# Rotating Strassen products over six PSUM tiles, starting two blocks of each group early, and moving the first batch's normaliser sums to another bank

## Chip, core and metric

The kernel runs on one core of one Trainium2 chip. The metric is the device time of one execution in microseconds (us). The kernel before was timed three times: 1553.96, 1553.99 and 1556.23 us, median 1553.99 us.

## What is computed

Attention with normalised queries and keys (8 batches, 12 heads, 448 positions, head size 64), and then a two-layer feed-forward with SiLU on the joined heads (3584 tokens, 768 to 2048 to 768). Everything is float32.

```python
q_n, k_n = rmsnorm(q, g_q), rmsnorm(k, g_k)
scores = (q_n @ k_n.T) / sqrt(64)
attn = exp(scores - max); attn = attn / (sum(attn) + 1e-9)
x = (attn @ v), heads joined: (3584, 768)
h = x @ w_in;  g = h * sigmoid(h);  out = g @ w_out
```

## The kernel before

The work is written out by hand in one order (a manual schedule), so every engine executes its instructions in the order in which the Python code emits them. Two arms are built; the data of this case takes the arm `bounded`.

**Pairs.** Batch and head pair give 48 pairs `n` (6 per batch `b`, numbered `hp` inside it). The main loop (L780) runs n = 0 to 48; n = 48 has no pair and only finishes. For each pair the loop emits, on TensorE: the first half of its scores (`scores(n, 0)`, L400), the second half of the weighted sum of the pair ahead (`weigh(n - 1, 1)`, L416), the transposes of the next queries (L381), a portion of filler work (`fill`, L803), the sums that normalise the pair ahead (`divide(n - 1)`, L445), the second half of the scores, the first half of the weighted sum, the transposes of the next keys (L386), and again filler (L841). ScalarE computes the exponentials (L405), copies transposed queries out of PSUM (L382), scales transposed keys of the first two batches (L390) and copies products; VectorE adds the exponentials (`add_up`, L430, L433), takes the reciprocal (L449), scales later keys (L392) and adds products (L459). GpSimd raises to a power (L304) and multiplies (L308, L451 for batch 0).

**Filler.** The first layer of the feed-forward is spread over the pairs as a generator: `begin(work, columns, parts)` sets a share of `columns / parts`, and each `fill()` emits matmuls until that share is used up. Batches 0 and 1 have eight of their blocks computed plainly (`whole`, L552, 6 matmuls a block); everything else goes by groups of two batches in Strassen-like blocks of seven products (`Seven`, L511), in the order 1, 2 (`two`) and 6, 5, 7, 3, 4 (`five`). Products 1 and 2 use the raw attention output; the others use sums that VectorE makes with `sum_x` (L456). A product's result is added or copied out of PSUM right after its last matmul, but the instruction for that is only emitted when the generator is resumed, which can be in the next portion. Rows of `stage` hold results; there are three such buffers, each block takes two.

**After the pairs.** The last group (batches 6 and 7) has no pairs beside it and runs alone (`alone = True`, L799), while `w_out` is loaded and rounded beside it (`prepare_out`, L674, instructions at L83, L84, L106 to L117). Then the second layer runs over 14 tiles of 256 tokens, again with seven products each (`halves_out`, L702).

**PSUM.** There are eight banks: two tiles `mm`, two tiles `sc` of two banks each (the scores of two heads), one `tr` (transposes and `divide`), one `av`. Beside pairs a product takes an `mm` tile. When alone, `bank()` (L481) walks through eight banks: mm, mm, sc half 0, sc half 1, sc half 0, sc half 1, tr, av; the two halves of an `sc` tile belong to one tile object.

Of the kernel before, what the change touches and what calls it, by code (L numbers as in the profile page):

```python
# [27 lines left out]
BANK = 512  # L28
# [296 lines left out]
def bounded(  # L325
# [112 lines left out]
    def divide(n):  # L438


        t = ps.tile([P, S], F32, name="tr")
        sums = [es, es_two] if n < z.NPAIR else [es]
        for i, part in enumerate(sums):
            for h in range(2):
                nc.tensor.matmul(  # L445
                    t[ds(h * D, D), :], ones[0:R, :], part[:, h, :],
                    start=i == 0, stop=i == len(sums) - 1,
                )
        nc.vector.reciprocal(out=r, in_=t)  # L449
# [284 lines left out]
    def fill(most=None):  # L734
        filler["due"] += filler["share"]
        while filler["due"] > 0 and most != 0:
            filler["due"] -= next(filler["work"], filler["due"])
            most = most and most - 1
# [3 lines left out]

    def finish():
        for _ in filler["work"]:
            pass
# [34 lines left out]
    for n in range(last + 2):  # L780
# [5 lines left out]
        if n > 0:  # L786
# [3 lines left out]
            unload(n - 1)  # L790
        transpose(n + 1, "q")
        if n == 0:
            normalise(2)
        if ends and n <= last:
            begin(halves_in([b - 2, b - 1], range(HF), plain), products,
                  4 * NPAIR - (2 if b == z.B - 2 else 1))
        weights_in(n, 0)
        if n > last:
            alone = True  # L799
            for _ in begun[1][1].two():  # L800
                pass
        else:
            fill(2 * HW if ends else None)  # L803
        weights_in(n, 1)
        if n == last:

            finish()
            rows = [staged() for _ in range(2)]
            begun = [(rows, part_in([b - 1, b], 0, rows))]
            rows = [staged(), work[:, 0 : 2 * S]]  # L810
            begun.append((rows, part_in([b - 1, b], 1, rows, kT)))
        if n > 0:
            divide(n - 1)
        if n <= last:
            scores(n, 1)
            weigh(n, 0)
        transpose(n + 1, "k")
        if n <= last:
            add_up(n, 1)
        if ends:  # L820
            sum_x([b - 2, b - 1], HW - 1)
            if n > last:
                begin(halves_in([b - 2, b - 1], range(HF), prepare_out, begun), 1, 1)
        elif hp == 0 and b == 1:
            begin(whole(0, early), len(early) * z.NW * S, 2 * NPAIR - 1)
        elif hp == 0 and b == 2:
            columns = len(early) * z.NW * S + products // 2
            begin(first_two(), columns, 4 * NPAIR - 2)
        weights_in(n, 2)
        if b % 2 == 1 and b > 1 and hp == NPAIR - 1:  # L830
            finish()
            for c in range(HW - 1):
                sum_x([b - 1, b], c)
            if n == last:
                for _ in begun[0][1].two():
                    pass
# [3 lines left out]
        elif n <= last:  # L840
# [220 lines left out]
```

## Time and profile before

The profiled execution took 1553.03 us, of which the instruction span is 1551.2 us.

| Part of the span (us) | What runs | Length | TensorE busy |
|---|---|---|---|
| 0 to 95.9 | start and batch 0, no filler | 95.9 | 68.3 |
| 95.9 to 860 | pairs with filler | 764.1 | 748.0 |
| 860 to 1016.9 | last group alone | 156.9 | 139.0 |
| 1016.9 to 1551.2 | second layer | 534.3 | 512.3 |

A float32 matmul stands in the trace as two records. A time in square brackets at a timeline row is the idle time of the engine ahead of the row and what ended it. `PEclk` is the clock that TensorE was granted, 1.00 being full.

### The profile page before, as it was taken

What the parts mean: (1) busy time and instruction counts of PE and PEld (TensorE: products, weight loads), DVE (VectorE), ACT (ScalarE), POOL (GpSimd) and SP (SyncE); (2) the same over time, 40 slices, a digit from 0 to 9 for tenths busy, and PEclk for the clock granted to TensorE, in tenths of its full rate; (3) what the DMA queues carried; (4) which work ended last, traced back from release to release, by engine and by line L of the source; (5) the groups of instructions that cost most, each with busy time, mean ns of one, the idle gap of its engine ahead of it and who ended that gap; (6) DMA issues with size and microseconds to landing.
All of it is one profiled execution on the core that took longest, in us unless ns stands there. A gap on an engine that the chain in (4) does not pass through costs nothing.

```text
span 1551.2 us, 14002 instructions
## 1 busy us (share of the span) xinstructions
PE 1467.5 (95%) x5072; PEld 704.4 (45%) x5072; DVE 739.8 (48%) x928; ACT 565.7 (36%) x931; POOL 393.7 (25%) x250
## 2 busy tenths in 40 slices
PE   5899999999899999899999989989999999999998
PEld 2334344434344444344444334455555555555554
DVE  4777776665755555755554766621211111222220
ACT  5778777444455454455454443300000000000000
POOL 5665341333233333313322133310000000000000
PEclk9999999999999999999999999999999999999999
DMA  6324332211222221222221246322222222222220
GB/s 199 106 67 139 109 99 66 66 60 54 60 84 60 60 83 60 60 66 71 60 72 36 77 164 210 119 78 74 75 75 80 75 80 75 75 76 85 81 68 23
DMA packets 119187, 128.94 MB, mean 83 GB/s; under 512 B 48836, under 2 KB 101316, under 8 KB 119108
## 3 DMA queue, kind: packets, MB, share of 16 engines
q1 hardware_dynamic: 118788, 127.95, 26.8%
q8 instruction: 42, 0.69, 0.2%
q14 instruction: 37, 0.30, 0.1%
q10 hardware_dynamic: 320, 0.00, 0.0%
HBM read 87.56 MB, written 40.37 MB: 82 GB/s over the span
## 4 chain that ended last, share of the span: by engine, by line
PE 84%; DVE 6%; issue 2%; ACT 1%; DMA 0%; POOL 0%; ACTq 0%; DVEq 0%; POOLq 0%
PE mm L511 28%; PE sc L511 19%; PE sc L400 9%; PE av L416 8%; PE tr L511 5%; PE av L511 5%; PE mm L552 5%; PE tr L445 3%; PE tr L386 1%; PE tr L381 1%; DVE work L433 1%; DVE sums_x L456 1%; DVE stage L459 1%; DVE parts L459 1%; DVE rms L298 0%
## 5 line engine op out<-in xcount | busy, mean ns | idle before, releaser
L405 ACT ACTIVATE work<-sc,rms 112x448 f32<-112x448 f32 x384 | 212.0, 635 | 226.9 <-PE sc L400 148.2
L304 POOL TENSOR_TENSOR rms<-rms,minus_half 112x16 f32<-112x16 f32 (+1 forms) x49 | 175.9, 3590 | 329.1 <-DVE rms L300 312.3
L511 PE MATMUL mm<-x,W 128*128 128x448 f32 x552 | 220.6, 542 | 1.3 <-DVE stage L459 0.9
L531 POOL TENSOR_TENSOR parts<-parts 128x448 f32<-128x448 f32 (+1 forms) x42 | 45.8, 1090 | 639.7 <-DVE parts L459 639.7
L449 DVE RECIPROCAL work<-tr 128x448 f32<-128x448 f32 x48 | 142.0, 2958 | 123.9 <-PE tr L445 112.5
L400 PE MATMUL sc<-work 64*112 64x448 f32 x768 | 173.0, 570 | 7.1 <-ACT work L390 4.7
L416 PE MATMUL av<-work,rows 112*64 112x448 f32 x768 | 165.5, 552 | 0.0
L511 PE MATMUL mm<-sums_x,W 128*128 128x448 f32 x384 | 157.0, 543 | 7.5 <-DVE stage L459 3.5
L433 DVE TENSOR_TENSOR work<-work 112x896 f32<-112x896 f32 x132 | 147.2, 1115 | 1.6
L511 PEld LDWEIGHTS mm<-x,W 128*128 128x128 f32 x552 | 101.8, 190 | 94.3 <-issue 87.2
L400 PEld LDWEIGHTS sc<-work 64*112 64x112 f32 x768 | 62.4, 176 | 107.4 <-issue 90.1
L511 PEld LDWEIGHTS mm<-sums_x,W 128*128 128x128 f32 x384 | 70.1, 190 | 73.0 <-issue 56.6
L511 PE MATMUL sc<-W,work 128*128 128x384 f32 x288 | 96.8, 486 | 0.0
L416 PEld LDWEIGHTS av<-work,rows 112*64 112x64 f32 x768 | 46.6, 136 | 109.0 <-issue 107.0
L459 DVE TENSOR_TENSOR stage<-mm,parts 128x448 f32<-128x448 f32 (+1 forms) x73 | 44.8, 617 | 104.2 <-PE mm L511 67.5
L459 DVE TENSOR_TENSOR parts<-mm,parts 128x448 f32<-128x448 f32 (+1 forms) x50 | 30.7, 613 | 112.4 <-PE mm L511 112.1
L552 PE MATMUL mm<-x,W 128*128 128x448 f32 x192 | 75.6, 541 | 0.0
L518 ACT COPY parts<-sc 128x384 f32<-128x384 f32 (+1 forms) x11 | 5.4, 493 | 190.6 <-PE sc L511 190.6
L511 PEld LDWEIGHTS sc<-W,work 128*128 128x128 f32 x288 | 54.8, 190 | 38.1
L459 DVE TENSOR_TENSOR parts<-sc,parts 128x384 f32<-128x384 f32 (+1 forms) x22 | 12.9, 584 | 104.5 <-PE sc L511 104.4
L405 ACT ACT_TABLE_LOAD x36 | 46.2, 1283 | 39.9 <-issue 36.9
L445 PE MATMUL tr<-work,ones 112*64 112x448 f32 x192 | 47.3, 572 | 13.3 <-ACT work L382 7.8
(146 smaller groups left out, 1883.6 us busy)
## 6 DMA issues: line engine op xcount, KB each, us to landing
hidden<-stage SPq DMA_DIRECT2D x55, 448.0 KB, 3.0
work<-hidden SPq DMA_DIRECT2D x7, 2048.0 KB, 9.4
x<-hidden SPq DMA_DIRECT2D x7, 2048.0 KB, 8.7
W<-in_moe_w_in_dram SPq DMA_DIRECT2D x24, 512.0 KB, 3.8
rows<-in_moe_w_out_dram SPq DMA_DIRECT2D x32, 384.0 KB, 3.8
rows<-in_q_dram SPq DMA_DIRECT2D x48, 224.0 KB, 3.5
rows<-in_k_dram SPq DMA_DIRECT2D x48, 224.0 KB, 3.3
rows<-in_v_dram SPq DMA_DIRECT2D x48, 224.0 KB, 2.6
```

Of the source, the lines that this page charges most:

```text
L304: nc.gpsimd.tensor_tensor(out=flat, in0=flat, in1=half, op=ALU.pow)
L381: nc.tensor.transpose(t[:, ts(j, R)], rows[:, j, :], ident[0:R, 0:R])
L400: nc.tensor.matmul(banks[:, h, 0:S], kT[rows, ts(j, R)], qT[n % 2][rows, :], start=True, stop=True,)
L405: nc.scalar.activation(e[j][:, h, :], banks[:, h, 0:S], AF.Exp, scale=rms[n % 4][:, 1, h, j : j + 1])
L416: nc.tensor.matmul(st["av"][ds(h * D, D), :], st["v"][:, h, j, :], e[j][:, h, :], start=(j == 0), stop=(j == J - 1),)
L433: nc.vector.tensor_tensor(out=es, in0=e[0] if j == 1 else es, in1=e[j], op=ALU.add)
L445: nc.tensor.matmul(t[ds(h * D, D), :], ones[0:R, :], part[:, h, :], start=i == 0, stop=i == len(sums) - 1,)
L449: nc.vector.reciprocal(out=r, in_=t)
L459: nc.vector.tensor_tensor(out=out, in0=a, in1=b, op=ALU.add)
L511: nc.tensor.matmul(t, self.left(name, s), self.right(name, s), start=s == ends[0], stop=s == ends[1])
L531: nc.gpsimd.tensor_tensor(out=u2, in0=u2, in1=p5, op=ALU.add)
L552: nc.tensor.matmul(h, room.w1(c, f), xT(b, c), start=(c == 0), stop=(c == z.NW - 1))
```

## The change

Four edits, in the order of the diff.

1. `divide` takes a `bank` (an `mm` tile, free in batch 0) in place of `tr` for the pairs of the first batch.
2. `bank()` in the alone stages walks through six tiles: mm, mm, sc, sc, tr, av. Of an `sc` tile only the first of the two banks is used.
3. For the groups that run beside pairs, `start` makes the first two blocks ahead: the products 1 and 2 of block 0 are emitted in the first portion of the group's first pair, ahead of `divide` (with their additions), and the products 1 and 2 of block 1 at the place of its second portion. `halves_in` goes on from there with the five other products. The first portion of `sum_x` stays at the end of the pair ahead, the second moves from there into the group's first pair. Block 1 keeps product 1 in the free half of its own row in place of `kT`, and its second row is a `stage` row.
4. The shares change: the plain blocks of batch 0 are spread over 12 portions in place of 11 (4 matmuls each), `first_two` over 23 in place of 22, the groups over 22 and 21 for 156 matmuls in place of 23 and 22 for 168. In batch 0 the transposes of the next keys are emitted ahead of the first half of the weighted sum.

```diff
     def divide(n):
-        t = ps.tile([P, S], F32, name="tr")
+        t = ps.tile([P, S], F32, name="tr") if n >= z.NPAIR else bank(S)
...
     alone = False
-    free_banks, shared = [], {}
+    order = ["mm", "mm", "sc", "sc", "tr", "av"]
 
     def bank(n):
         if not alone:
             return ps.tile([P, BANK], F32, name="mm", bufs=2)[:, 0:n]
-        if not free_banks:
-            free_banks.extend([("mm", [P, BANK], None)] * 2)
-            free_banks.extend([("sc", [P, 2, BANK], i) for i in range(2)] * 2)
-            free_banks.extend((name, [P, S], None) for name in ("tr", "av"))
-        name, shape, half = free_banks.pop(0)
-        if half != 1:
-            bufs = 2 if name in ("mm", "sc") else 1
-            shared["bank"] = ps.tile(shape, F32, name=name, bufs=bufs)
-        t = shared["bank"]
-        return t[:, 0:n] if half is None else t[:, half, 0:n]
+        name = order[0]
+        order.append(order.pop(0))
+        if name == "sc":
+            return ps.tile([P, 2, BANK], F32, name=name, bufs=2)[:, 0, 0:n]
+        if name == "mm":
+            return ps.tile([P, BANK], F32, name=name, bufs=2)[:, 0:n]
+        return ps.tile([P, S], F32, name=name)[:, 0:n]
...
-                columns, skip = part.five(int(m == 0)), 5 * (HW - 1) if m == 0 else 0
+                late = int(alone and m == 0)
+                columns, skip = part.five(late), 5 * (HW - late) * late
...
+    def start(group):
+        begun = []
+        for m in range(2):
+            rows = [staged() for _ in range(2)]
+            begun.append((rows, part_in(group, m, rows, rows[0][:, S:] if m else None)))
+        return begun
...
             unload(n - 1)
+            if ends and n <= last:
+                sum_x([b - 2, b - 1], 1)
         transpose(n + 1, "q")
...
+        weights_in(n, 0)
         if ends and n <= last:
-            begin(halves_in([b - 2, b - 1], range(HF), plain), products,
-                  4 * NPAIR - (2 if b == z.B - 2 else 1))
-        weights_in(n, 0)
-        if n > last:
+            begun = start([b - 2, b - 1])
+            run(begun[0][1].two())
+        elif n > last:
             alone = True
-            for _ in begun[1][1].two():
-                pass
+            run(begun[1][1].two())
         else:
-            fill(2 * HW if ends else None)
+            fill()
...
         if n <= last:
             scores(n, 1)
+        if b == 0:
+            transpose(n + 1, "k")
+        if n <= last:
             weigh(n, 0)
-        transpose(n + 1, "k")
+        if b > 0:
+            transpose(n + 1, "k")
...
             sum_x([b - 2, b - 1], HW - 1)
+            group = [b - 2, b - 1]
             if n > last:
-                begin(halves_in([b - 2, b - 1], range(HF), prepare_out, begun), 1, 1)
+                run(halves_in(group, range(HF), prepare_out, begun))
+            else:
+                run(begun[1][1].two())
+                begin(halves_in(group, range(HF), plain, begun), products - 4 * HW * S,
+                      4 * NPAIR - (3 if b == z.B - 2 else 2))
         elif hp == 0 and b == 1:
-            begin(whole(0, early), len(early) * z.NW * S, 2 * NPAIR - 1)
+            begin(whole(0, early), len(early) * z.NW * S, 2 * NPAIR)
         elif hp == 0 and b == 2:
             columns = len(early) * z.NW * S + products // 2
-            begin(first_two(), columns, 4 * NPAIR - 2)
+            begin(first_two(), columns, 4 * NPAIR - 1)
...
-            for c in range(HW - 1):
-                sum_x([b - 1, b], c)
+            sum_x([b - 1, b], 0)
             if n == last:
-                for _ in begun[0][1].two():
-                    pass
+                sum_x([b - 1, b], 1)
+                run(begun[0][1].two())
...
-        elif n <= last:
+        elif not ends:
             fill()
```

The order of instructions moves as follows; `L511` before and `L508` after are the same line, a product's matmul.

TensorE in batch 0, before: from the transposes of one pair's keys to the scores of the same pair's second half (`tr`, `sc`, `av`, `mm` are PSUM tiles, `rows` and `qn` the loaded and normalised inputs).

```order
L386 MATMUL tr<-ident,rows 128x112 x4
L400 MATMUL sc<-work 112x448 x4
L416 MATMUL av<-work,rows 64x448 x4
L381 MATMUL tr<-ident,qn_103 128x112 x4
L445 MATMUL tr<-work,ones 64x448 x2
L445 MATMUL tr<-stage,ones 64x448 x2
L400 MATMUL sc<-work 112x448 x4
```

The same place in the changed kernel, from the second half of the scores of the pair ahead.

```order
L400 MATMUL sc<-work 112x448 x4
L386 MATMUL tr<-ident,rows 128x112 x4
L416 MATMUL av<-work,rows 64x448 x4
L400 MATMUL sc<-work 112x448 x4
L416 MATMUL av<-work,rows 64x448 x4
L381 MATMUL tr<-ident,qn_103 128x112 x4
L445 MATMUL mm<-work,ones 64x448 x2
L445 MATMUL mm<-stage,ones 64x448 x2
```

A weighted sum (L416) now stands between the key transposes and the scores that use the keys, and the sums of `divide` (L445) no longer write the tile that the query transposes have just filled.

TensorE around the start of group 2, 3 (n = 23 to 24), before, from the key transposes at the end of pair 23.

```order
L386 MATMUL tr<-ident,rows 128x112 x4
L400 MATMUL sc<-work 112x448 x4
L416 MATMUL av<-work,rows 64x448 x4
L381 MATMUL tr<-ident,qn_103 128x112 x4
L511 MATMUL mm<-x_144,W 128x448 x6
L445 MATMUL tr<-work,ones 64x448 x2
L400 MATMUL sc<-work 112x448 x4
L416 MATMUL av<-work,rows 64x448 x4
L386 MATMUL tr<-ident,rows 128x112 x4
L511 MATMUL mm<-sums_x,W 128x448 x6
```

The same place in the changed kernel.

```order
L386 MATMUL tr<-ident,rows 128x112 x4
L508 MATMUL mm<-x_143,W 128x448 x2
L508 MATMUL mm<-sums_x,W 128x448 x3
L400 MATMUL sc<-work 112x448 x4
L416 MATMUL av<-work,rows 64x448 x4
L381 MATMUL tr<-ident,qn_103 128x112 x4
L508 MATMUL mm<-x_144,W 128x448 x6
L445 MATMUL tr<-work,ones 64x448 x2
L400 MATMUL sc<-work 112x448 x4
L416 MATMUL av<-work,rows 64x448 x4
L386 MATMUL tr<-ident,rows 128x112 x4
L508 MATMUL mm<-x_144,W 128x448 x6
```

Five matmuls of the group ahead now stand between the key transposes and the scores, and the second portion of pair 24 uses raw outputs (`x_144`) and no longer sums (`sums_x`).

TensorE at the start of the second layer, before, with tile numbers: four products in a row of the first token tile (`x0_143` and `W_75` hold weights, `work_148` the tokens).

```order
L511 MATMUL mm_4800<-x0_143,work_148 128x384 x2
L511 MATMUL mm_4800<-W_75,work_148 128x384 x6
L511 MATMUL sc_4810<-x0_143,work_148 128x384 x2
L511 MATMUL sc_4810<-W_75,work_148 128x384 x6
L511 MATMUL sc_4810<-x0_143,work_148 128x384 x2
L511 MATMUL sc_4810<-W_75,work_148 128x384 x6
L511 MATMUL sc_4831<-x0_143,work_148 128x384 x2
L511 MATMUL sc_4831<-W_75,work_148 128x384 x6
```

Products at the same stage in the changed kernel.

```order
L508 MATMUL mm_4794<-x0_143,work_148 128x384 x2
L508 MATMUL mm_4794<-W_75,work_148 128x384 x6
L508 MATMUL sc_4804<-x0_143,work_148 128x384 x2
L508 MATMUL sc_4804<-W_75,work_148 128x384 x6
L508 MATMUL sc_4814<-x0_143,work_148 128x384 x2
L508 MATMUL sc_4814<-W_75,work_148 128x384 x6
L508 MATMUL tr_4824<-x0_143,work_148 128x384 x2
L508 MATMUL tr_4824<-W_75,work_148 128x384 x6
```

Two products in a row shared the tile object `sc_4810`; now each product has one of its own, and the next tile to come round is six products away.

More of the change, by code (lines that the diff above doesn't have):

```diff
@@ L732, in begin, with fill, run @@
         filler.update(work=work, due=0.0, share=columns / parts)
-    def fill(most=None):
+    def fill():
         filler["due"] += filler["share"]
-        while filler["due"] > 0 and most != 0:
+        while filler["due"] > 0:
             filler["due"] -= next(filler["work"], filler["due"])
-            most = most and most - 1
     def plain(m):
         yield
+    def run(work):
+        for _ in work:
+            pass
     def finish():
-        for _ in filler["work"]:
-            pass
+        run(filler["work"])
+    def start(group):
[4 more added lines that the diff above has]
+        return begun
     early, late = range(z.NF // 2), range(HF // 2, HF)
@@ L807, in bounded @@
             finish()
[L808 to L811, printed above, removed]
+            begun = start([b - 1, b])
         if n > 0:
```

1 line of the change is left out of this document (removed).

## The prediction

> **What bounds the kernel now.** I read the stages first (busy time by windows), since the page's 95% of TensorE is a mean over unlike stages.
>
> ```profile
> span 1551.2 us, 14002 instructions
> ```
>
> ```profile
> 95.90:860.00 764.10, 748.02 (x2826) 317.27 (x2824) 472.85 (x560) 432.13 (x686) 252.70 (x136) 1.00 0.23 71
> ```
>
> ```profile
> 1016.92:1545.50 528.58, 512.27 (x1569) 296.03 (x1567) 103.91 (x126) 14.34 (x29) 27.24 (x28) 1.00 0.24 73
> 873.89:1016.92 143.03, 125.10 (x314) 60.03 (x313) 92.70 (x155) 49.87 (x90) 52.42 (x48) 0.96 0.44 143
> ```
>
> The columns are the length, then busy time and count of TensorE, its weight loads, VectorE, ScalarE and GpSimd, the granted clock, the DMA share and GB/s. Beside the pairs TensorE is busy 748 of 764 us. In the second layer it is busy 512 of 529 us while VectorE needs 104, and in the last group 125 of 143 us while VectorE needs 93. TensorE is the limit in all three, so each gap on it counts in full and no other engine fills a stage. The gaps are named by the view of waits, TensorE alone; first the last group (860 to 1017 us), then the second layer.
>
> ```profile
> PE sc L511 <- DVE stage L459: 9.8, 5, 4.2
> PE sc L511 <- DVE parts L459: 5.0, 5, 2.0
> PE sc L511 <- ACT parts L529: 1.9, 2, 1.3
> PE sc L511 <- ACT parts L518: 1.2, 2, 0.6
> ```
>
> ```profile
> PE sc L511 <- DVE stage L459: 4.2, 6, 0.7
> PE sc L511 <- DVE parts L459: 4.1, 6, 0.7
> PE sc L511 <- DVE W L459: 3.4, 5, 0.7
> PE sc L511 <- ACT parts L518: 2.4, 4, 0.6
> PE sc L511 <- ACT parts L529: 2.2, 3, 0.9
> ```
>
> Every wait of these two stages is on an `sc` tile: 14 waits with 17.9 us, and 24 with 16.3 us. None is on `mm`, `tr` or `av`. The same view over the whole run names the rest, all ahead of 860 us.
>
> ```profile
> PE tr L386 <- POOL rms L304: 12.2, 1, 12.2
> PE tr L445 <- ACT work L382: 7.8, 6, 2.0
> PE sc L400 <- ACT work L390: 4.7, 6, 0.8
> PE mm L511 <- DVE stage L459: 4.4, 5, 1.4
> PE tr L445 <- DVE W L106: 3.3, 1, 3.3
> PE mm L511 <- DVE sums_x L456: 2.9, 2, 1.5
> PE tr L445 <- DVE work L433: 2.2, 2, 1.1
> PE sc L400 <- DVE work L392: 1.7, 2, 0.9
> ```
>
> The first row is the start of the kernel, which the change leaves alone. Batch 0 loses 12.5 us (the second and third row); the fifth is one gap in pair 12; the other four are 11.2 us at the starts of the groups and in the filler of batches 2 and 3.
>
> **Second layer: one product for each `sc` tile.** The timeline of TensorE, one group of products:
>
> ```profile
> 1075.57 1.45 PE L511 MATMUL mm<-x,x 128*128 128x384 f32 x4
> 1080.73 1.46 PE L511 MATMUL sc<-x,sums_x 128*128 128x384 f32 x4
> 1086.78 1.56 PE L511 MATMUL sc<-x,x 128*128 128x384 f32 x4 [0.72 <-DVE stage L459]
> 1092.04 1.45 PE L511 MATMUL sc<-x,work 128*128 128x384 f32 x4
> 1097.97 1.56 PE L511 MATMUL sc<-x,work 128*128 128x384 f32 x4 [0.61 <-ACT parts L518]
> 1103.24 1.46 PE L511 MATMUL tr<-x,work 128*128 128x384 f32 x4
> ```
>
> ```profile
> 1086.16 0.56 DVE L459 TENSOR_TENSOR stage<-sc,parts 128x384 f32<-128x384 f32 x1 [4.62 <-PE sc L511]
> ```
>
> From `mm` to `sc` a product takes 1080.73 - 1075.57 = 5.16 us. The next, into the second half, starts 6.05 us later: it waits until the first half has been read at 1086.16 to 1086.72, though that read touches another bank. The order with tile numbers says why: both halves are one tile object (`sc_4810`). Four products from 1080.73 to 1103.24 take 22.51 us, where four of 5.16 are 20.64: 1.87 lost, more than the 1.33 of idle, because the first matmuls after a gap run 1.56 and not 1.45.
>
> The stage has 14 token tiles of 7 products, 98 in all (1569 records at 16 each). 98 x 5.16 = 505.7 us against 528.6 in the window: **22.9 us** go, if no new wait comes. In the new rotation a product waits for the reading of the one six before it, with five others in between, 5 x 5.16 = 25.8 us. The longest VectorE has to do in one piece there, the four sums of the next token tile, is far below that (104 us in 14 tiles, 7.4 us for everything). The lower end is 20, if an eighth of the gaps stays under another name.
>
> The Trainium skill ("TensorE: Matmul & The Clock Gate", section "A second HAM failure mode: psum-queue depth-cycling") says that frequent small idle spells between groups of matmuls, when products cycle through PSUM banks, make the clock oscillate between half and full. By that rule the products behind the 24 gaps would run at half speed now, and up to 24 x 5.16 = 124 us more would be won, an estimate from its rule and the product above. The trace does not agree: the row of this stage has the clock at 1.00 with all 24 gaps in it, and the sum goes by the row.
>
> **Last group.** 1569 and 314 records show the size: 52 products of six records. Unstalled neighbours:
>
> ```profile
> 890.82 2.42 PE L511 MATMUL mm<-sums_x,W 128*128 128x448 f32 x6
> 893.08 2.42 PE L511 MATMUL mm<-x,W 128*128 128x448 f32 x6
> 901.95 4.85 PE L511 MATMUL sc<-sums_x,W 128*128 128x448 f32 x6 [4.20 <-DVE stage L459]
> ```
>
> ```profile
> 908.07 0.62 DVE L459 TENSOR_TENSOR work<-sc,parts 128x448 f32<-128x448 f32 x1
> ```
>
> A product takes 2.26 us, so 52 take 117.5, and 25.5 us is the most to win. It exceeds the 17.9 us of idle because the product behind the longest gap ran 4.85 instead of 2.42. Here VectorE also rounds `w_out` and falls behind: block 1's last addition comes at 908.07 and ends at 908.7. That bank (`av`) is wanted again six products later. With five products begun at 873.9 and ten more, TensorE comes to it at 873.9 + 15 x 2.26 = 907.8: a wait of about 1 us. After that VectorE's 92.7 us in the window are below the 117.5 that TensorE needs, so it catches up. I take 2 us off for this and other remnants: **23.5 us**, between 12 (VectorE, ScalarE and the loads of `w_out` make a chain of their own) and 25.5.
>
> **Batch 0.** Two gaps a pair:
>
> ```profile
> 69.69 2.96 DVE L449 RECIPROCAL work<-tr 128x448 f32<-128x448 f32 x1 [2.84 <-POOL rms L304]
> 77.27 1.09 DVE L430 TENSOR_TENSOR stage<-work 112x896 f32<-112x896 f32 x1
> ```
>
> ```profile
> 79.35 0.97 PE L445 MATMUL tr<-work,ones 112*64 112x448 f32 x4 [1.16 <-ACT work L382]
> 80.15 0.92 PE L445 MATMUL tr<-stage,ones 112*64 112x448 f32 x4
> 81.00 1.76 PE L400 MATMUL sc<-work 64*112 64x448 f32 x8
> 90.86 0.97 PE L445 MATMUL tr<-work,ones 112*64 112x448 f32 x4 [1.17 <-ACT work L382]
> ```
>
> The 1.16 is `divide` waiting until ScalarE has copied the queries out of the one `tr` tile; an `mm` tile is free at once. The 0.78 (4.7 over six) is the scaling of the keys, now covered by a weighted sum. A pair lasts 90.86 - 79.35 = 11.51 us; without both gaps it would be 9.6. But then VectorE binds: from the reciprocal's start to the end of the addition that `divide` needs is 77.27 + 1.09 - 69.69 = 8.67 us, then the second half of `divide` (0.92) and two hand-overs of about 0.1: a circle of 9.8. So 1.7 a pair for four pairs, and about 3 for the first two, whose wait for `tr` was the longest (2.0): **10 us**, between 6 (a longer circle) and 12.5 (all idle).
>
> **Pair 12.** Eleven portions used up the plain blocks, and the twelfth was empty:
>
> ```profile
> 183.18 1.68 PE L445 MATMUL tr<-work,ones 112*64 112x448 f32 x4 [3.29 <-DVE W L106]
> 184.78 2.70 PE L400 MATMUL sc<-work 64*112 64x448 f32 x8
> ```
>
> Besides the 3.29, these rows took 1.68 and 2.70 where the same work took 0.97 and 1.76 above: 1.65 more. Twelve portions of 4 matmuls put 4 here (3 us), so I take **4.6 us** of 4.9, at least 3.
>
> **Starts of groups and filler.** The remaining four rows sum to 11.2 us. At pairs 24 and 36 the key scaling (1.7 for both) is covered by five or more filler matmuls; the wait for the exponentials' sums (2.2) goes since one portion of `sum_x` now stands behind them; the wait for `sum_x` (2.9) goes since the second portion needs no sums. The 4.4 for an `mm` tile come where a portion of filler ends exactly on a product, so that its addition is only emitted with the next portion; with 23 shares fewer do. I take **10**, between 0 (others appear, since the shares shift everything) and 11.2. The added `stage` row makes block 1 wait for block 0's store; that is how all later blocks work, and I cost it at nothing: five products lie between.
>
> **Sum.** 22.9 + 23.5 + 10 + 4.6 + 10 = 71.0 us from the profiled 1553.0: 1482.0. The median of the three runs lies 1.0 above that execution, so I forecast **1483 us**. All upper ends together (22.9 + 25.5 + 12.5 + 4.9 + 11.2 = 77.0) give 1477, and 1476 if matmuls behind a gap of batch 0 lost another 1 us as in pair 12. All lower ends together (41) give 1513; the causes are unrelated, so I take the half of it for the forecast's own range, 1494.
>
> **Rivals.**
>
> *The last group is set by another chain* (15 in 100). Rounding a piece needs its load, two ScalarE and three VectorE instructions, and additions queue between them. For it: the gap of 4.20 ended with VectorE late, not TensorE. Against: 93 of 143 us. If the stage gains 12 or less, the time is 1494 to 1506.
>
> *Fewer banks, more bubbles* (3 in 100). If the gaps came from the number of banks, six in place of eight would bring them 8/6 as often: 22.9 becomes 30.5 and 25.5 becomes 34, a loss of 16 against the other gains of 25, about 1545. It is also the case in which the change does not do what it says. Against: no gap at the single tiles `mm`, `tr` and `av`. The Trainium skill has that rule ("Perfetto Trace Analysis", section "Optimization Strategy": the same gap again and again can mean that there are too few buffers); the rows above do not agree with it here.
>
> *Slower: the clock* (2 in 100). If TensorE without gaps were granted less, the whole run stretches: each 0.01 costs 15 us, and below 0.95 it is slower than before; at 0.93 it is 1595. Against: 748 busy of 764 us at 1.00.
>
> The forecast has the remaining 80 in 100, its own range 1476 to 1494. With the first rival's nearer half the range is **1476 to 1500**. A measurement here tells apart about 0.2%, 3 us. Faster by more: 0.95; within: 0.02 (parts undone by waits not seen); slower: 0.03.
>
> **What would show it.** Right: no wait on `sc` L508 in the second layer and 5.16 us a product throughout; the last group's 52 products in about 119.5 us; in batch 0 reciprocals 9.8 us apart; no gap of 3 us at pair 12; under 3 us of waits of `mm`, `tr` and `sc` from 96 to 860 us. Wrong: gaps at `tr` or `av` tiles in the last group with VectorE late, or a clock below 1.00 in the second layer.

## The result and the profile after

The changed kernel takes 1479.2 us (median of four runs: 1476.25, 1479.0, 1479.38 and 1479.56), the kernel before beside it 1554.1 us (median of four). The ratio is 0.951, 95% interval 0.949 to 0.953: 4.9% faster, 74.9 us. The forecast was 1483 us in a range of 1476 to 1500.

The profiled execution of after is the fastest of the four, 1476.25 us. The stages are compared through it and the 1553.03 us of before, a difference of 76.8 us. The page and the view by windows of after, cut at the same places of the program as before (first filler product; first product of the stage alone; first product of the second layer; last product):

```profile
span 1474.5 us, 14016 instructions
```

```profile
84.64:844.08 759.44, 758.03 (x2867) 321.67 (x2865) 483.87 (x574) 441.93 (x699) 253.28 (x137) 1.00 0.24 75
```

```profile
32.17:84.64 52.47, 51.90 (x260) 18.53 (x261) 47.31 (x50) 42.60 (x81) 44.16 (x23) 1.00 0.38 102
844.08:962.74 118.66, 117.76 (x315) 59.28 (x314) 91.47 (x153) 48.89 (x89) 50.14 (x46) 1.00 0.53 169
962.74:1468.60 505.86, 505.84 (x1569) 297.98 (x1567) 105.33 (x129) 15.18 (x30) 29.46 (x30) 1.00 0.25 78
```

The same view of before, for batch 0 from 32.17 us on and for the pairs with filler (the table ahead of the prediction cuts both elsewhere):

```profile
32.17:96.30 64.13, 54.38 (x269) 19.81 (x265) 47.91 (x50) 43.25 (x81) 45.59 (x24) 0.97 0.32 89
96.30:873.89 777.59, 761.51 (x2867) 322.44 (x2865) 483.47 (x574) 440.49 (x699) 252.30 (x136) 1.00 0.24 73
```

| Stage (lengths in us) | Before | After | Gain | Forecast |
|---|---|---|---|---|
| start and batch 0, to the first filler product | 96.30 | 84.64 | 11.7 | 10 |
| pairs with filler | 777.6 | 759.4 | 18.2 | 14.6 (pair 12: 4.6; the rest: 10) |
| last group | 143.0 | 118.7 | 24.4 | 23.5 |
| second layer | 528.6 | 505.9 | 22.7 | 22.9 |

From the first filler product to the last product TensorE is busy 1381.6 of 1384.0 us, and the work of the other engines has hardly changed: VectorE's 92.7 us of the last group are 91.5 now. The gain is waiting time of TensorE, and in part matmuls that ran slowly behind a wait. The view of waits shows what is left of it, TensorE over the whole run of after:

```profile
PE tr L386 <- POOL rms L304: 12.3, 1, 12.3
PE tr L381 <- POOL qn L308: 1.6, 2, 1.3
PE av L508 <- DVE stage L459: 0.9, 1, 0.9
PE tr L381 <- ACT work L390: 0.8, 1, 0.8
PE mm L445 <- DVE stage L430: 0.8, 1, 0.8
PE mm L508 <- ACT parts L515: 0.6, 1, 0.6
...
```

The first row is the start, which the change leaves alone. No row names an `sc` tile with a product (L508). The one wait of the last group is on `av`, with 0.9 us. The timeline of TensorE in the second layer has 5.16 us from product to product, through `mm`, `sc`, `sc` and `tr` alike:

```profile
967.90 1.45 PE L508 MATMUL mm<-x,work 128*128 128x384 f32 x4
...
973.06 1.45 PE L508 MATMUL sc<-x,work 128*128 128x384 f32 x4
...
978.22 1.45 PE L508 MATMUL sc<-x,work 128*128 128x384 f32 x4
...
983.38 1.45 PE L508 MATMUL tr<-x,work 128*128 128x384 f32 x4
```

### The profile page after: what moved, and what is told of

It is laid out like the page before. It is cut to its first block, busy times and chain, and to the rows that moved or that the text cites. A ratio compares the mean times of both kernels' runs of the same rounds, so it can differ in the third digit from the quotient of the medians.

```text
span 1474.5 us, 14016 instructions
## 1 busy us (share of the span) xinstructions
PE 1449.3 (98%) x5072; PEld 703.8 (48%) x5072; DVE 739.8 (50%) x928; ACT 566.2 (38%) x931; POOL 393.4 (27%) x250
## 4 chain that ended last, share of the span: by engine, by line
PE 92%; DVE 5%; issue 1%; DMA 1%; ACT 0%; POOL 0%; ACTq 0%; SPq 0%; DVEq 0%; POOLq 0%
PE mm L508 35%; PE sc L508 13%; PE sc L400 9%; PE av L416 9%; PE av L508 7%; PE tr L508 7%; PE mm L549 5%; PE tr L445 3%; PE tr L386 1%; PE tr L381 1%; DVE work L449 1%; DVE rms L298 1%; DVE work L433 0%; DVE W L109 0%; DMA W<-in_moe_w_in_dram 0%
## 5 line engine op out<-in xcount | busy, mean ns | idle before, releaser
L304 POOL TENSOR_TENSOR rms<-rms,minus_half 112x16 f32<-112x16 f32 (+1 forms) x49 | 175.8, 3588 | 290.9 <-DVE rms L300 271.6
L508 PE MATMUL mm<-x,W 128*128 128x448 f32 x552 | 220.9, 541 | 0.7 <-ACT parts L515 0.6
L449 DVE RECIPROCAL work<-tr 128x448 f32<-128x448 f32 x42 | 124.2, 2957 | 104.5 <-PE tr L445 104.3
L400 PE MATMUL sc<-work 64*112 64x448 f32 x768 | 170.7, 563 | 1.0 <-ACT work L382 0.6
L508 PE MATMUL mm<-sums_x,W 128*128 128x448 f32 x408 | 165.9, 542 | 0.7 <-DVE stage L459 0.4
L416 PE MATMUL av<-work,rows 112*64 112x448 f32 x768 | 165.5, 552 | 0.0
L508 PEld LDWEIGHTS mm<-x,W 128*128 128x128 f32 x552 | 101.9, 190 | 93.0 <-issue 87.9
L400 PEld LDWEIGHTS sc<-work 64*112 64x112 f32 x768 | 61.3, 173 | 103.8 <-issue 82.8
L508 PEld LDWEIGHTS mm<-sums_x,W 128*128 128x128 f32 x408 | 74.9, 190 | 68.9 <-issue 61.4
L416 PEld LDWEIGHTS av<-work,rows 112*64 112x64 f32 x768 | 46.6, 136 | 105.3 <-issue 103.8
L508 PE MATMUL mm<-W,work 128*128 128x384 f32 x204 | 68.6, 486 | 0.0
L515 ACT COPY parts<-mm 128x448 f32<-128x448 f32 (+1 forms) x27 | 14.1, 523 | 141.7 <-PE mm L508 141.7
L508 PE MATMUL sc<-W,work 128*128 128x384 f32 x192 | 64.5, 486 | 0.0
L634 ACT ACTIVATE stage<-stage 128x896 f32<-128x896 f32 x56 | 50.7, 944 | 31.7 <-DVE stage L459 26.0
L298 DVE TENSOR_REDUCE rms<-qn 112x8 f32<-112x512 f32 x49 | 33.3, 680 | 44.8 <-ACT qn L297 44.7
```

The costliest lines, as they stand in the source:

```text
L298: nc.vector.tensor_reduce(out=rms[:, i], in_=t, axis=AX.X, op=ALU.add)
L304: nc.gpsimd.tensor_tensor(out=flat, in0=flat, in1=half, op=ALU.pow)
L400: nc.tensor.matmul(banks[:, h, 0:S], kT[rows, ts(j, R)], qT[n % 2][rows, :], start=True, stop=True,)
L416: nc.tensor.matmul(st["av"][ds(h * D, D), :], st["v"][:, h, j, :], e[j][:, h, :], start=(j == 0), stop=(j == J - 1),)
L508: nc.tensor.matmul(t, self.left(name, s), self.right(name, s), start=s == ends[0], stop=s == ends[1])
L634: nc.scalar.activation(t, t, AF.Silu)
```

## Experiments

Each run was timed beside the kernel before on its own chip (1554.45, 1554.35 and 1553.3 us in the three series). A time is a median, with the lowest and highest run in brackets; a ratio has its 95% interval. Differences go by 1479.2 us for the changed kernel; measured again in the last series it took 1477.65, so 1.5 us between two series is not a difference. Unless said otherwise, edits are to the changed kernel.

**The rotation alone.** The kernel before, with only edit 2 of the change:

```diff
-    free_banks, shared = [], {}
+    order = ["mm", "mm", "sc", "sc", "tr", "av"]
     def bank(n):
...
+        name = order[0]
+        order.append(order.pop(0))
+        if name == "sc":
+            return ps.tile([P, 2, BANK], F32, name=name, bufs=2)[:, 0, 0:n]
```

> The kernel before with one edit of the change alone: the new rotation, one product for each sc tile. Theory (the waits on sc come from two products in one tile object): the second layer falls from 528.6 to 505.8 us and the last group from 143.0 to about 118.7, as in the changed kernel, and nothing else moves: 1554.1 - 47.1 = 1507 us (1504 to 1510). Rival 1 (part of the last group's gain comes from the third row of stage that block 1 now has): the last group stays above 124 us, 1512 or more. Rival 2 (the gaps come from the number of banks): six banks in place of eight, 1540 or more.

Measured: 1509.3 us (1508.6 to 1510.1), ratio 0.971 (0.969 to 0.973). The two stages by windows, last group and second layer:

```profile
876.50:995.13 118.63, 117.89 (x314) 59.22 (x313) 90.81 (x154) 48.60 (x89) 50.18 (x46) 1.00 0.52 169
995.13:1500.97 505.84, 505.84 (x1569) 297.73 (x1567) 105.34 (x129) 15.21 (x30) 29.46 (x30) 1.00 0.25 78
```

They are as long as in the changed kernel. So the whole gain of these stages is the rotation's, and the third `stage` row has no part in it. The median lies 2 us above the forecast, inside its range. In the profiled execution (1508.78 us) the part ahead of the last group took 876.50 us for 873.89 in before, though the edit touches nothing there: the first wait of TensorE was 13.3 us for 12.2, one wait of batch 0 was 1.6 us for 0.8, and some matmuls behind waits ran more slowly.

**Halves of one tile, but far apart.** Is it the shared tile object, the second half, or the number of banks?

```diff
-    order = ["mm", "mm", "sc", "sc", "tr", "av"]
+    order = ["a0", "b0", "mm", "mm", "a1", "b1", "tr", "av"]
+    shared = {}
...
+            if name[1] == "0":
+                shared[name[0]] = ps.tile([P, 2, BANK], F32, name="sc", bufs=2)
+            return shared[name[0]][:, int(name[1]), 0:n]
```

> The changed kernel with eight banks again: both halves of the sc tiles take products, but the second half of a tile comes four products after its first (first half A, first half B, mm, mm, second half A, second half B, tr, av). Theory (a shared tile object costs only where its second half is wanted before the first has been read): no wait on sc in the second layer, 5.16 us a product, 1479 us (1476 to 1482). Rival 1 (the wait is bound to the second half, or to two halves of one tile in any order): 24 gaps again, 1495 or more. Rival 2 (more banks help by themselves): the wait of 0.9 us on av goes too, which is below what the times can tell.

Measured: 1479.75 us (1479.2 to 1481.6). The second layer by windows has no idle time, with eight banks and both halves in use:

```profile
965.89:1471.70 505.81, 505.81 (x1569) 298.21 (x1567) 105.33 (x129) 15.18 (x30) 29.45 (x30) 1.00 0.25 78
```

So in the second layer a shared tile as such costs nothing. In before it cost 1.87 us in every rotation, because its second half was wanted one product after the first, ahead of the reading of the first. What the rotation of six won there was not fewer or more banks, but that no two successive products share a tile.

In the last group, where VectorE is later, the shared tile still costs something: the stage takes 120.5 us for 118.7, and two waits on `sc` stand in place of the one on `av`.

```profile
862.46 2.52 PE L511 MATMUL sc<-x,W 128*128 128x448 f32 x6 [1.02 <-DVE stage L459]
...
882.18 2.52 PE L511 MATMUL sc<-x,W 128*128 128x448 f32 x6 [1.41 <-DVE stage L459]
```

By the order of products both write the first half of a new B tile, and both wait until VectorE has read the second half of the B tile before it, four products earlier (it reads from 861.80 to 862.41 us and from 881.51 to 882.13). At 882.18 the bank that is wanted was itself last written at 862.46 and read from 868.91 on. So these waits too are those of two halves in one object, and eight banks gave this order no more room than the three products in between.

**Two banks.** The other end, from the third block of the last group on:

```diff
+        taken.append(n)
+        if len(taken) > 12:
+            return ps.tile([P, BANK], F32, name="mm", bufs=2)[:, 0:n]
         name = order[0]
```

> The changed kernel, with a rotation of two mm banks in place of six from the third block of the last group on (the two begun blocks need theirs). Theory (what counts is how late the reader is, not the number of banks): in the second layer a product takes 5.16 us and VectorE is never later than the four left sums, 4.8 us, so even two banks lose nothing there, 505.8 to 508 us. In the last group VectorE has rounding and right sums of up to 4 us in one piece queued between the additions, against 2.26 us of a product, so there it costs about 14 us (5 to 25): 1493 us in all (1484 to 1506). Rival (fewer banks, more bubbles everywhere): the second layer at 520 or more, 1505 or more in all.

Measured: 1503.2 us (1502.7 to 1504.0), 24 more than the changed kernel. The waits of TensorE in the last group (846 to 989 us), and then by windows the matmuls right behind five of them (waits of 1.92, 5.02, 3.04, 3.06 and 3.42 us) and the second layer:

```profile
PE mm L511 <- DVE parts L459: 9.5, 3, 3.4
PE mm L511 <- DVE stage L459: 5.0, 1, 5.0
PE mm L511 <- ACT parts L518: 1.9, 1, 1.9
PE mm L511 <- ACT parts L529: 1.7, 2, 0.8
```

```profile
874.38:876.90 2.52, 2.52 (x6) 1.05 (x6) 1.60 (x4) 0.80 (x1) 1.55 (x1) 1.00 0.65 169
881.92:886.38 4.46, 4.46 (x6) 2.18 (x7) 4.08 (x8) 1.96 (x5) 1.70 (x3) 0.52 0.87 279
909.88:913.94 4.06, 4.06 (x6) 1.88 (x7) 0.62 (x1) 0.00 (x0) 2.21 (x2) 0.58 0.93 293
947.58:951.63 4.05, 4.05 (x7) 2.01 (x7) 0.62 (x1) 0.00 (x0) 2.21 (x2) 0.58 0.00 0
985.63:989.45 3.82, 3.82 (x7) 1.89 (x8) 0.63 (x1) 0.95 (x1) 2.22 (x2) 0.61 0.03 13
989.45:1495.30 505.85, 505.84 (x1569) 297.73 (x1567) 103.92 (x126) 14.36 (x29) 27.23 (x28) 1.00 0.25 78
```

The second layer needs two banks and no more: 505.85 us. The rival (fewer banks, more bubbles) is out. The whole run loses 24 us by the medians, which is inside the expected total (1484 to 1506); the last group itself takes 144.4 us (845.01 to 989.45) for 118.7, 25.8 more where 14 and at most 25 were expected: 18.1 us of waits, and the rest behind them. I had left that rest out: behind the four long waits the clock column has 0.52 to 0.61, and a product takes 3.8 to 4.5 us, where it takes 2.52 behind the wait of 1.92. VectorE shows why it is late at 881.92, in its timeline:

```profile
875.00 0.95 DVE L456 TENSOR_TENSOR x<-x 128x768 f32<-128x768 f32 x1
876.84 2.69 DVE L456 TENSOR_TENSOR x<-x 128x768 f32<-128x768 f32 x3 [0.89 <-POOL x L117]
879.45 0.62 DVE L459 TENSOR_TENSOR stage<-av,parts 128x448 f32<-128x448 f32 x1
...
881.25 0.62 DVE L459 TENSOR_TENSOR stage<-mm,parts 128x448 f32<-128x448 f32 x1
```

The first two rows are the right sums for `w_out`, 4.5 us with their own wait for GpSimd; two additions whose products were ready stand behind them, with 1.3 us of rounding between the two, and the `mm` tile is free at 881.9. The six banks of the changed kernel cover all but 0.9 us of the same delay.

**The beginnings of the groups undone.** Edits 3 and 4 taken back but for the keys of batch 0; rotation and sums as changed:

```diff
-            begun = start([b - 2, b - 1])
-            run(begun[0][1].two())
+            begin(halves_in([b - 2, b - 1], range(HF), plain), products,
+                  4 * NPAIR - (2 if b == z.B - 2 else 1))
```

> The changed kernel with the beginnings of the groups and the shares of the filler as before; the rotation, the sums of batch 0 and the keys' place stay as changed. Theory: the 18.2 us that the middle (from the first filler to the last group) gained come back, 1479.2 + 18.2 = 1497 us (1494 to 1500), with a gap of about 3 us at pair 12 again; the second layer stays at 505.8 and batch 0 at 9.77 us a pair. Rival (the middle's gain comes in part from batch 0's edits, since the shares begin earlier): 1491 or less.

Measured: 1496.4 us (1495.3 to 1498.1), 17.2 more than the changed kernel. The waits from 84 to 862 us are those of before, row for row; the largest:

```profile
PE mm L508 <- DVE stage L459: 4.4, 5, 1.4
PE tr L445 <- DVE W L106: 3.3, 1, 3.3
PE mm L508 <- DVE sums_x L456: 2.9, 2, 1.5
```

Three runs thus make a sum: rotation 45.1 us (1554.45 to 1509.3), batch 0 12.9 (1509.3 to 1496.4), groups and shares 17.2, together 75.2. They add up by their making, since each run puts one part on top of the one ahead; the order in which the parts are put on could shift some of it between them.

**The shares alone undone.** The plain blocks over 11 portions and `first_two` over 22 again; the beginnings of later groups as changed:

```diff
-            begin(whole(0, early), len(early) * z.NW * S, 2 * NPAIR)
+            begin(whole(0, early), len(early) * z.NW * S, 2 * NPAIR - 1)
...
-            begin(first_two(), columns, 4 * NPAIR - 1)
+            begin(first_two(), columns, 4 * NPAIR - 2)
```

> The changed kernel with the filler of the first two rounds divided by one share fewer each (by 11 and 22 in place of 12 and 23); the beginnings of the later groups stay as changed. Theory: the filler is used up one portion early, the gap of 3.3 us at pair 12 with 1.65 us of matmuls at half speed behind it is back, 4.9 us, and the five waits on mm between 255 and 360 us come back in part (0 to 4.5): 1479.2 + 6 = 1485 us (1484 to 1489). Rival (the gap at pair 12 is only shifted to the end of the next round, or the waits there are all from the groups' beginnings): 1479 to 1482.

Measured: 1489.1 us (1488.4 to 1489.8), 9.9 more, at the upper end of the range. The timeline of TensorE has the gap at pair 12 and the waits on `mm`:

```profile
172.88 1.76 PE L445 MATMUL tr<-work,ones 112*64 112x448 f32 x4 [3.30 <-DVE W L106]
...
263.86 2.52 PE L508 MATMUL mm<-sums_x,W 128*128 128x448 f32 x6 [1.41 <-DVE stage L459]
...
```

So 9.9 of the 17.2 us are lost by two numbers in the code alone, 11 for 12 and 22 for 23, with the beginnings of the groups as changed. The shares as changed without those beginnings were not run.

**Batch 0, its two edits apart.** First the sums back in `tr`, with the keys where the change put them:

```diff
-        t = ps.tile([P, S], F32, name="tr") if n >= z.NPAIR else bank(S)
+        t = ps.tile([P, S], F32, name="tr")
```

> The changed kernel with the first batch's sums back in the one tr tile; the keys' transposition stays ahead of the weighted sum. Theory (VectorE's circle of 9.77 us and TensorE's 9.6 us a pair lie close, so each wait that comes back costs nearly in full): the wait for ScalarE's copy of the queries returns, 1.16 us a pair and 2.0 for the first; reciprocals about 10.75 us apart, and about 6 us more in all: 1485 us (1483 to 1487). Rival (VectorE's circle hides it, and the keys' place alone gave batch 0 its gain): reciprocals stay at 9.8 us, 1479 to 1481.

Measured: 1488.1 us (1487.2 to 1489.6), 8.9 more, 1.1 us above the range. The wait that I had expected is shorter than I thought, and one that I had not seen is there:

```profile
72.03 0.60 PE L386 MATMUL tr<-ident,rows 112*128 112x112 f32 x4 [1.44 <-DVE work L449]
...
78.78 0.97 PE L445 MATMUL tr<-work,ones 112*64 112x448 f32 x4 [0.62 <-ACT work L382]
```

With the keys ahead of the weighted sum, their transposition wants the one `tr` tile while the reciprocal (2.96 us) still reads the sums in it. So moving the keys ahead pays only with the sums elsewhere: with both back, as in before, a pair took 11.51 us, and here 78.78 less 67.17 (the same row one pair ahead), 11.6. Then the keys behind the weighted sum, with the sums in `mm`:

```diff
-        if b == 0:
-            transpose(n + 1, "k")
         if n <= last:
             weigh(n, 0)
-        if b > 0:
-            transpose(n + 1, "k")
+        transpose(n + 1, "k")
```

> The changed kernel with the first batch's keys transposed behind the weighted sum again; the sums stay in an mm tile. Theory: the wait of 0.78 us for the scaled keys returns, TensorE needs 9.6 + 0.8 = 10.4 us a pair, 0.6 more than now; reciprocals 10.4 us apart and about 3.5 us more in all: 1482.7 us (1481 to 1484.5). Rival (VectorE's circle of 9.77 us sets the pair and hides the keys): reciprocals stay at 9.8, within 1 us of 1479.2.

Measured: 1481.3 us (1478.7 to 1481.7), 2.1 more. The times alone hardly tell that apart, but in its timeline the wait is back (`sc` L400, 0.79 us, each pair), and a pair takes 10.27 us:

```profile
67.83 1.76 PE L400 MATMUL sc<-work 64*112 64x448 f32 x8 [0.79 <-ACT work L390]
...
78.10 1.76 PE L400 MATMUL sc<-work 64*112 64x448 f32 x8 [0.79 <-ACT work L390]
```

That is 0.5 a pair over the 9.77 of the changed kernel, since VectorE's circle covers the rest of the 0.79: the theory's direction, with less than its 0.6.

**The start.** The largest wait left is the first one, 12.3 us. The trace puts it down to GpSimd's power (L304), but VectorE computes the choice between the two arms (L250 to L254) only behind the scaled queries, by its timeline in the changed kernel:

```profile
10.18 0.69 DVE L308 TENSOR_TENSOR qn<-rows,rms 112x512 f32<-112x512 f32 x1 [1.71 <-POOL rms L304]
...
11.27 0.14 DVE L254 TENSOR_SCALAR small<-most 1x1 int32<-1x1 f32 x1
```

The edit tried there belongs to no part of the change:

```diff
+    for i, g in enumerate((g_q, g_k)):
+        nc.sync.dma_start(g1[:, i, :], g.rearrange("(one d) -> one d", one=1))
     load(state, 0)
...
     load(state, 1)
-    for i, g in enumerate((g_q, g_k)):
-        nc.sync.dma_start(g1[:, i, :], g.rearrange("(one d) -> one d", one=1))
```

> The changed kernel with one edit at the start, where TensorE idles 12.3 us in its longest wait: the two loads of the gains' rows, on which the choice between the two arms of the program rests, are issued ahead of the loads of queries and keys in place of behind them. Theory (the wait that the profile puts down to GpSimd's power ends when the choice is known, at 11.4 us, since VectorE computes it only then): the first transposition moves from 12.3 to about 7 us, and the second, which needs the scaled queries of 10.9 us, from 14.05 to about 11.6: 2.5 us less, 1476.7 us (1475 to 1478). Rival (the wait is on GpSimd's power as the view says, or the later load of the queries delays what follows): no gain, 1479 or more.

Measured: 1479.15 us (1477.9 to 1479.7): nothing won. The timeline of TensorE shows that the theory held for the first 4 us, and that the gain was lost again:

```profile
7.53 0.98 PE L386 MATMUL tr<-ident,rows 112*128 112x112 f32 x4 [7.53 <-DVE rms L300]
10.21 0.98 PE L381 MATMUL tr<-ident,qn 112*128 112x112 f32 x4 [1.70 <-DVE qn L308]
...
27.41 3.33 PE L400 MATMUL sc<-work 64*112 64x448 f32 x8 [6.70 <-ACT work L390]
```

The 6.70 is put down to ScalarE's scaling of the keys, but ScalarE was itself waiting. The timeline of all engines:

```profile
6.22 5.50 SPq L68 DMA_DIRECT2D W<-in_moe_w_in_dram  x8
...
12.84 0.34 SPq L218 DMA_DIRECT2D rows<-in_q_dram  x1
...
22.86 0.63 ACT L297 ACTIVATE qn<-rows 112x512 f32<-112x512 f32 x1 [5.47 <-DMA rows<-in_q_dram]
```

The queries that ScalarE wants at 22.86 were asked for at 12.84 us, behind eight loads of weights of 512 KB. Of the two rivals that the expectation names, the second held: the load of the queries was late for what follows. So the next run moves the weights, on top of that edit:

```diff
-    while room.w_in.load():
-        pass
+    for _ in range(2):
+        room.w_in.load()
```

> The run with the gains' rows first, with one edit more: only two of the first nine pieces of the weights are asked for at the start, the other seven behind the loads of the third and fourth pair's queries and keys. Theory (there the first pair began 4 us earlier, and all of it was lost again because ScalarE waited until 22.9 us for the third pair's queries, whose load stood behind 4 MB of weights): the wait of 6.7 us in front of the second pair's scores goes, batch 0 begins 3 to 4 us earlier, 1475.5 us (1474 to 1477), under both kernels. Rival (the pairs' own chain through GpSimd's power sets the beginning, whatever is loaded when): no better than the changed kernel, 1478 or more.

The expectation says nine pieces where it should say eight at first; the ninth is loaded later in both kernels. Measured: 1473.0 us (1472.0 to 1473.4), ratio to before 0.948 (0.947 to 0.949). Two runs beside it on the same chip say what that is worth: the weights later without the early choice, and the changed kernel again.

> The changed kernel with the seven weight loads behind the loads of the third and fourth pair, and the gains' rows where they were. Theory: as long as the first pair begins at 12.3 us no load of queries is late, so nothing is won: 1479.2 us, within 1.5. Rival (the weights hold up the start by themselves): 1477 or less.

> The changed kernel itself, on the same chip as the two runs on its start, since 3 us are to be told apart: 1479.2 us, within 1.

Measured: 1476.95 us (1476.1 to 1478.2) and 1477.65 us (1476.5 to 1478.8, ratio 0.951 as at first). Both expectations were missed: the first lies just below the rival's 1477, and the changed kernel itself came 1.55 us below its 1479.2. So the rival's mark does not count for it: beside the changed kernel of the same series the weights alone win 0.7 us, and the runs overlap. With the choice made early they win 4.6 us by the medians, and the runs of the two kernels do not overlap; the two profiled executions, 1476.52 and 1473.35 us, are 3.2 apart. Whether the queries were late for their place behind the weights or for the bandwidth that the weights took is not told apart. The timeline of TensorE has the scores of the second pair at 23.05 us without a wait, where they stood at 27.41 with the early choice alone and at 25.22 in the changed kernel:

```profile
23.05 1.76 PE L400 MATMUL sc<-work 64*112 64x448 f32 x8
```

This is the fastest version of the study, faster than both kernels.

## Why the prediction was right, and where its sizes were off

**Second layer: 22.9 against 22.7.** The mechanism and the size were read from one group of products, and the length of 98 products of 5.16 us (505.7) is what the window shows (505.86, and 505.84, 505.81 and 505.85 in three experiments). The Trainium skill ("TensorE: Matmul & The Clock Gate", section "A second HAM failure mode: psum-queue depth-cycling") has small idle spells between groups of matmuls make the clock oscillate, and by that rule products would have become shorter once the gaps were gone. Here a product takes 5.16 us without any gap, as the ones with no gap ahead did in before. One reason in the prediction's working is too small: the 1.87 us lost a rotation exceeds the idle 1.33 by 0.54, of which the longer first matmuls (1.56 for 1.45) are only 0.22. The other 0.32 is overlap: in an unbroken row a product begins 0.16 us ahead of the modelled end of the one before it (by its rows the product at 1103.24 ends at 1104.53 + 4.03 = 1108.56, and the next begins at 1108.40), and each of the two waits loses that too.

**Last group: 23.5 against 24.4.** The wait at `av` came where it was worked out, 0.9 us for about 1:

```profile
879.20 2.52 PE L508 MATMUL av<-x,W 128*128 128x448 f32 x6 [0.90 <-DVE stage L459]
```

It is the sign that the prediction named as wrong, an `av` tile with VectorE late, at the size that its sum had allowed for. After it VectorE caught up, so the second microsecond that I took off for remnants was not needed. The prediction puts the excess of 25.5 over 17.9 us down to the one product of 4.85. That is a third of it. The 24.4 gained are 17.0 of waits, 4.1 of the two products behind the waits of 4.20 and 3.30 (4.85 and 4.06 for 2.42), and for the thirteen waits fewer 2.1 of lost overlap and some 1.1 of rows of 2.52 for 2.42. The rival in which another chain sets this stage did not happen: VectorE's last addition of block 1 begins at 878.53 us, 11.5 after its product (TensorE comes back to the tile at 878.3, five products of 2.26 after that product's end, 867.0), and six banks are 0.9 us short of hiding it. With two banks that rival is real, as the run shows.

**Batch 0: 10 against 11.7.** The circle of VectorE was worked out as 9.8 us and is 9.77:

```profile
61.49 2.96 DVE L449 RECIPROCAL work<-mm 128x448 f32<-128x448 f32 x1 [1.14 <-PE mm L445]
...
71.27 2.96 DVE L449 RECIPROCAL work<-mm 128x448 f32<-128x448 f32 x1 [1.15 <-PE mm L445]
```

Four pairs at 1.74 make the 7 that I had; the first two pairs and their waits gave 4.7, for which I took 3. The term that was short is the matmuls behind the first wait, in before:

```profile
31.70 0.97 PE L445 MATMUL tr<-work,ones 112*64 112x448 f32 x4 [1.98 <-ACT work L382]
...
33.53 3.23 PE L400 MATMUL sc<-work 64*112 64x448 f32 x8
```

The scores take 3.23 us for 1.76, and the sums between the two rows 1.09 for 0.92: 1.6 us more, at a granted clock of 0.71 to 0.75 from 31.70 to 38.00. The prediction had such matmuls at pair 12, and for batch 0 only as 1 us in its upper bound. What the prediction did not see is that its two edits are not independent: the keys' move was costed as 0.78 covered, and by itself, with the sums in `tr`, it brings a wait of 1.44.

**Pair 12 and the groups: 14.6 against 18.2.** This is the term that was mis-sized. The gap at pair 12 went, with its 4.9. For the rest I had 11.2 us from four rows of waits, and took 10. Two rows of the same view were left out of the list (0.9 and 0.3), so the idle time was 12.4; 1.2 of other waits are left after (0.6, 0.4 and 0.2, all on `mm`), and the net is 11.2. A product behind a short wait runs 2.52 and not 2.42, some 0.1 each for nine waits of before and three of after. With pair 12 that makes 16.7. The other 1.5 us is about what ten waits fewer (three for thirteen) save in overlap, at 0.16 each: the idle time of the two windows falls by 14.7 us (16.1 to 1.4) and the busy time by 3.5. So what failed in size was to count the idle time of four rows alone. How the gain splits between the shares and the beginnings I had not said; 9.9 us is measured for the shares, and some 7 for the beginnings is only what is left.

**Sum.** 71.0 forecast and 76.8 in the profiled executions; by the medians 74.9. The profiled execution of after lies 3 us below its median, so some 2 us of the gains by stage are its own, and which stage has them is not known. Every term but the second layer's came out above its taken value and inside its own bounds, except the groups, whose 13.3 (18.2 less 4.9) lies over the upper bound of 11.2. No term made up for another, so the total is not luck. The rival with the clock did not come: it is 1.00 in all three stages without gaps. Two numbers at the prediction's end do not follow from its own working: the two small chances are exchanged (the rival at 1545 us, 3 in 100, is hardly faster than before, and the one with the clock, 2 in 100, is the slower one), and 1494 is near the middle of 1476 and 1513, not half of the shortfall from 1483, which would give 1498.

## What to carry to other kernels

When an engine waits at a buffer of which others are free, look at which tile object it is: in these runs two halves of one object were one buffer for the order. That costs as soon as one half is wanted before the other has been read, which a stage with a late reader shows even when the halves stand four products apart. How many buffers a rotation needs is set by how late the reader can be against the length of one product, so it is read stage by stage: here two suffice in one stage, and six leave a wait in the other. A wait that is removed at the start pays only if the next load is there in time; look what is queued ahead of that load before the wait goes.

## What the runs showed of the hardware

Once the work was under way, the granted clock was lower after every wait of 3 us or more, and after some of 2 us. In the run with two banks, waits of up to 1.9 us left the granted clock of the next six matmuls at 1.00 (2.52 us for them); waits of 3.0, 3.1, 3.4 and 5.0 us were followed by 0.52 to 0.61 (3.8 to 4.5 us). In the last group of before, a wait of 2.05 us left it at 1.00 (886.96 to 890.80 us), and waits of 3.30 and 4.20 us were followed by 0.60 and 0.50. In the run with the gains first, a wait of 6.70 us was followed by 0.50 (27.41 to 30.70 us). But in batch 0 waits of 1.96 to 1.98 us were followed by 0.71 to 0.75 in before, by 0.53 with the rotation alone (33.63 to 37.00 us) and by 0.55 with the sums in `tr` (32.43 to 36.00 us). There, shorter waits of 0.2 to 1.6 us stand close ahead. So the length of one wait does not decide alone, and what decides at 2 us is not shown. The first wait of a run is left out: in after the column has 1.00 behind it, yet the first eight matmuls of the scores, from 15.68 us on, took 3.33 us, where eight from 20.86 us on took 1.76. The Trainium skill ("TensorE: Matmul & The Clock Gate", section "Why this matters for your kernels") asks for no idle gaps of more than about 3 us between bursts of matmuls; the rows from 3.0 us on agree, and those of batch 0 lost clock at 2.0.

What a wait costs is more than its idle time. In the run with two banks, the product behind the wait of 3.04 us was due at 906.68 us (two products of 2.26 after 902.17) and the next at 908.94. The next began at 913.94: 5.0 us late, which are the 3.04, the 0.16 of overlap and 1.8 of slow matmuls. The wait of 1.92 us cost 2.2. This is in part why the view of waits shows less than is to be won: the 17.9 us of waits in the last group of before went together with 24.4 us of its length.
